# How the second product's columns are shared out over four column tiles of TensorE: 1, 2, 2, 1 matmuls in place of 1, 1, 1, 3

One core of one Trainium2 chip (trn2). The metric is the device time of the whole kernel in microseconds, from the first to the last instruction; lower is better. The run before takes 2520 us.

## The reference

A short causal convolution over time with one 7-tap filter for each of 8 heads, then a feed-forward block without bias, in fp32. The core of it:

```python
def reference(x, weight, w_in, w_out):        # x (8, 4096, 192), weight (8, 7)
    w = softmax(weight, axis=-1)
    out[b, s, h, g] = sum_k w[h, k] * x_pad[b, s + k, h, g]      # 6 zeros ahead of each sequence
    h = out.reshape(32768, 192) @ w_in                           # w_in (192, 2048)
    g = h * (1 / (1 + exp(-1.702 * h)))
    return g @ w_out                                             # w_out (2048, 192)
```

## The kernel before

It computes both matrix products by a Strassen-like scheme of sums and fewer block products. The work is cut in 64 stages of 512 tokens in two halves. Each stage has product 1 (with `w_in`), the activation on ScalarE, sums on VectorE, and then the second product: seven block products, each 96 output features (three chunks of 32) by 256 tokens, accumulated over 1024 rows of weights, 8 steps of 128.

TensorE is used as four column tiles of 128 x 32. A tile writes 32 partitions of PSUM, and one block product is 3 x 256 = 768 columns of 32 partitions, so 192 for each tile. The part that matters, cut and with comments added (`Q` = 32, `TA` = 192, `TB` = 64, `NK` = 8):

```python
def product2(slot, bank, a, b, first=True):
    dst = slot[:, bank, 0:TA]
    for j in range(NK):
        for c in range(3):                      # tiles 0, 1, 2: tokens 0 to 191 of chunk c
            nc.tensor.matmul(dst[c * Q : (c + 1) * Q, :],
                w_out_s[:, a, j, c * Q : (c + 1) * Q], g[:, b, j, 0:TA],
                start=(first and j == 0), stop=(j == NK - 1), skip_group_check=True)
        for c in range(3):                      # tile 3: tokens 192 to 255 of all three chunks
            nc.tensor.matmul(dst[3 * Q :, c * TB : (c + 1) * TB],
                w_out_s[:, a, j, c * Q : (c + 1) * Q], g[:, b, j, TA:T],
                start=(first and j == 0 and c == 0), stop=(j == NK - 1), skip_group_check=True)
    return dst

# ... in output(s, last, work): seven calls of product2, each followed by a copy on ScalarE
# or sums and 32 x 32 transposes on VectorE, then the transfers out:
for c in range(3):
    nc.sync.dma_start(out=rows[c, :, 0 : TA // Q, :], in_=osb[c * Q : (c + 1) * Q, n, :, :])
    nc.sync.dma_start(out=rows[c, :, TA // Q :, :],
                      in_=osb[3 * Q :, n, c * TB // Q : (c + 1) * TB // Q, :])
```

The call of `nc.tensor.matmul` loads its weights and multiplies. In fp32 each call shows up in the trace as two weight loads and two matmuls: 64 stages x 7 products x 8 steps x 6 calls are 21504 calls, and the trace has 43008 such matmuls. A "round" in all that follows is six matmuls of the trace, so there are 16 rounds in a block product and 112 in a stage.

## Time and profile before

| | before |
|---|---|
| median of 6 runs, us | 2520.47 (2517.91 to 2521.54) |
| span of the profiled run, us | 2520.6 |
| TensorE on the chain that ended last | 96% |
| second product on that chain | 47% |
| one stage of the second product, median | 18.90 us |

A stage of the second product is counted here from its first matmul to the first matmul of product 1 after it. The lines of the page and of the timeline are in the prediction. The end of the stage that the prediction reads, in the timeline of the kernel before (start in us, duration, engine, line):

```profile
1061.77 0.34 PE L445 MATMUL slot<-g,w_out_s 128*32 128x192 f32 x3
1061.80 0.50 PE L455 MATMUL slot<-g,w_out_s 128*32 128x64 f32 x6
1062.23 0.92 PE L350 MATMUL sums<-f,w_in_s 64*128 64x256 f32 x6
```

Tiles 0 to 2 are through with their last matmuls while tile 3 still has six of its own to go: three of the round before and three of the last. The stage ends with tile 3.

### The profile page before, as it was taken

To read this page: it belongs to the slowest core of one execution; us is meant where nothing else is said; L and a number is where in the kernel's file an instruction comes from. 1 tells how busy PE (TensorE), PEld (TensorE's weight loads), DVE (VectorE), ACT (ScalarE), POOL (GpSimd) and SP (SyncE) were. 2 spreads that over 40 slices of the span, in tenths; PEclk is the share of its full clock that TensorE was granted. 3 is DMA by queue.
4 is the path that set the end of the run, shared out by engine and by line. 5 is a ranking of instruction groups with operands and counts; after the bars stand their busy time and mean duration, and the time that the engine had idled before them with its cause. 6 is when DMAs were issued, how large, how long until landed. Compare 5 with 4: busy or idle time off the path is not lost.

```text
span 2520.6 us, 114341 instructions
## 1 busy us (share of the span) xinstructions
PE 2478.5 (98%) x54336; PEld 2303.3 (91%) x54336; DVE 1714.2 (68%) x2370; ACT 952.5 (38%) x1060; POOL 4.8 (0%) x20
## 2 busy tenths in 40 slices
PE   8889999999999999999999999999999999999998
PEld 5779999999999999999999999999999999999998
DVE  7856667666667666667666676666676666677654
ACT  6224334334334334334343343343343343343342
POOL 0000000000000000000000000000000000000000
PEclk9999999999999999999999999999999999999999
DMA  7122212212212222122122122122122222121110
GB/s 165 32 56 53 57 31 54 57 34 55 55 31 57 44 47 57 42 44 56 39 51 57 33 52 58 36 54 56 28 58 47 43 57 49 38 57 39 28 34 15
DMA packets 197603, 123.43 MB, mean 49 GB/s; under 512 B 115984, under 2 KB 191248, under 8 KB 193168
## 3 DMA queue, kind: packets, MB, share of 16 engines
q1 hardware_dynamic: 197120, 116.13, 21.9%
q8 instruction: 424, 6.95, 1.1%
q14 instruction: 43, 0.35, 0.0%
q10 hardware_dynamic: 16, 0.00, 0.0%
HBM read 53.15 MB, written 25.17 MB: 31 GB/s over the span
## 4 chain that ended last, share of the span: by engine, by line
PE 96%; DVE 1%; ACT 1%; DMA 1%; issue 0%; SPq 0%; DVEq 0%; ACTq 0%
PE slot L350 30%; PE slot L455 30%; PE sums L350 18%; PE slot L445 17%; PE slot L527 0%; DVE g L439 0%; ACT g L373 0%; DMA f<-f 0%; DMA xin<-in_x_dram 0%; ACT u L390 0%; DVE xt L296 0%; ACT f L198 0%; SPq L102 0%; ACT f L197 0%; ACT f L195 0%
## 5 line engine op out<-in xcount | busy, mean ns | idle before, releaser
L455 PE MATMUL slot<-g,w_out_s 128*32 128x64 f32 x21504 | 1219.6, 219 | 1.1 <-issue 0.8
L445 PE MATMUL slot<-g,w_out_s 128*32 128x192 f32 x21504 | 1209.6, 330 | 10.4 <-DVE w_out_s L257 9.9
L455 PEld LDWEIGHTS slot<-g,w_out_s 128*32 128x32 f32 x21504 | 1205.9, 110 | 2.7 <-issue 1.9
L350 PE MATMUL slot<-f,w_in_s 64*128 64x256 f32 x7168 | 843.9, 378 | 11.5 <-DMA f<-f 10.4
L350 PEld LDWEIGHTS slot<-f,w_in_s 64*128 64x128 f32 x7168 | 691.7, 188 | 100.5 <-DMA f<-f 11.2
L439 DVE TENSOR_TENSOR g<-g 128x1024 f32<-128x1024 f32 x512 | 609.5, 1222 | 191.9 <-ACT g L373 187.5
L445 PEld LDWEIGHTS slot<-g,w_out_s 128*32 128x32 f32 x21504 | 629.5, 108 | 34.2 <-issue 23.4
L350 PE MATMUL sums<-f,w_in_s 64*128 64x256 f32 x4096 | 515.1, 380 | 5.8 <-ACT sums L383 3.0
L390 ACT COPY u<-sums 128x1024 f32<-128x1024 f32 x128 | 129.5, 1012 | 1029.6 <-PE sums L350 1029.6
L350 PEld LDWEIGHTS sums<-f,w_in_s 64*128 64x128 f32 x4096 | 392.3, 187 | 56.7 <-ACT sums L383 3.7
L313 DVE SCALAR_TENSOR_TENSOR f<-xt,cw,f 128x512 f32<-128x512 f32 x558 | 417.5, 748 | 14.2
L373 ACT ACTIVATE g<-u 128x1024 f32<-128x1024 f32 x256 | 269.7, 1054 | 14.2 <-DVE u L430 14.1
L430 DVE TENSOR_TENSOR u<-u,slot 128x1024 f32<-128x1024 f32 x128 | 155.9, 1218 | 68.6 <-PE slot L350 68.6
L420 DVE TENSOR_TENSOR u<-u,slot 128x1024 f32<-128x1024 f32 x128 | 155.7, 1216 | 68.4 <-ACT u L403 65.5
L493 DVE TENSOR_TENSOR u<-u,slot 128x192 f32<-128x192 f32 x64 | 22.7, 355 | 247.7 <-PE slot L455 247.7
L403 ACT COPY u<-sums 128x1024 f32<-128x1024 f32 x128 | 129.6, 1012 | 133.7 <-PE sums L350 133.7
L373 ACT ACTIVATE g<-sums 128x1024 f32<-128x1024 f32 x128 | 130.6, 1020 | 94.7 <-PE sums L350 94.7
L373 ACT ACTIVATE g<-slot 128x1024 f32<-128x1024 f32 x128 | 131.5, 1027 | 45.0 <-PE slot L350 45.0
L383 ACT COPY sums<-slot 128x1024 f32<-128x1024 f32 x128 | 128.8, 1006 | 27.9 <-PE slot L350 25.8
L489 DVE TENSOR_TENSOR u<-u,slot 128x192 f32<-128x192 f32 x64 | 22.7, 354 | 99.6 <-PE slot L455 99.6
L483 ACT COPY u<-slot 128x192 f32<-128x192 f32 x64 | 20.4, 319 | 159.0 <-PE slot L455 159.0
L473 DVE STREAM_TRANSPOSE osb<-u 128x192 f32<-128x192 f32 x192 | 72.3, 376 | 4.4
(57 smaller groups left out, 417.5 us busy)
## 6 DMA issues: line engine op xcount, KB each, us to landing
xin<-in_x_dram SPq DMA_DIRECT2D x240, 180.0 KB, 4.5
f<-f SPq DMA_DIRECT2D x62, 576.0 KB, 4.8
out_dram<-osb SPq DMA_DIRECT2D x384, 48.0 KB, 1.7
out_dram<-osb SPq DMA_DIRECT2D x384, 16.0 KB, 1.5
g<-in_moe_w_in_dram SPq DMA_DIRECT2D x8, 384.0 KB, 9.4
g<-in_moe_w_out_dram SPq DMA_DIRECT2D x4, 768.0 KB, 5.1
xin<-in_x_dram SPq DMA_DIRECT2D x16, 160.0 KB, 3.2
f<-f SPq DMA_DIRECT2D x2, 256.0 KB, 3.4
```

Of the source, the lines that this page charges most:

```text
L313: vec.scalar_tensor_tensor(out=dst, in0=src, scalar=tap, in1=dst, op0=ALU.mult, op1=ALU.add)
L350: nc.tensor.matmul(slot[:, h, j * T : (j + 1) * T], w_in_s[halves[h], u, a, j * P : (j + 1) * P], f[halves[h], 0 if h == o else 1, b, :], ...
L373: act.activation(g[:, b, j : j + NK // NU, :].rearrange("p f t -> p (f t)"), src.rearrange("p h n -> p (h n)"), AF.Gelu_apprx_sigmoid,)
L383: act.copy(sums, self.x)
L390: act.copy(self.u2, sums)
L403: act.copy(self.u3, sums)
L420: vec.tensor_add(self.u3, self.u3, self.z)
L430: vec.tensor_add(self.u2, self.u2, self.z)
L439: vec.tensor_sub(v[dst], v[a], v[b])
L445: nc.tensor.matmul(dst[c * Q : (c + 1) * Q, :], w_out_s[:, a, j, c * Q : (c + 1) * Q], g[:, b, j, 0:TA], start=(first and j == 0), stop=(j ...
L455: nc.tensor.matmul(dst[3 * Q :, c * TB : (c + 1) * TB], w_out_s[:, a, j, c * Q : (c + 1) * Q], g[:, b, j, TA:T], start=(first and j == 0 a ...
L473: vec.transpose(osb[:, n, :, m * Q : (m + 1) * Q], src.rearrange("p (j t) -> p j t", t=Q),)
```

## The change

The 768 columns become one row, which is cut in four equal parts: a tile takes 192 consecutive columns. Two of the cuts fall inside a tile, so tiles 1 and 2 have two matmuls each, and no tile has three. The output transfers follow the new places.

```diff
-    TB = T - TA
+    # tile, chunk, first token, tokens, first column in the tile
+    LANES = [
+        (0, 0, 0, TA, 0),
+        (1, 0, TA, T - TA, 0),
+        (2, 1, T // 2, T // 2, 0),
+        (3, 2, T - TA, TA, 0),
+        (1, 1, 0, T // 2, T - TA),
+        (2, 2, 0, T - TA, T // 2),
+    ]
     for j in range(NK):
-        for c in range(3): ...  # 192 tokens of chunk c on tile c
-        for c in range(3): ...  # 64 tokens of chunk c on tile 3
+        for l, c, t, n, at in LANES:
+            nc.tensor.matmul(dst[l * Q : (l + 1) * Q, at : at + n],
+                w_out_s[:, a, j, c * Q : (c + 1) * Q], g[:, b, j, t : t + n],
+                start=(first and j == 0 and at == 0), stop=(j == NK - 1), skip_group_check=True)
```

(The diff is shortened: the removed calls are named by their comments, the comment on the fields is added here, and the transfers, cut away, loop over `LANES` in the same way.) The intent is that the slowest tile has less to do beside its columns.

More of the change, by code (lines that the diff above doesn't have):

```diff
@@ L443, in product2 @@
         for j in range(NK):
-            for c in range(3):
+            for l, c, t, n, at in LANES:
                 nc.tensor.matmul(
-                    dst[c * Q : (c + 1) * Q, :],
+                    dst[l * Q : (l + 1) * Q, at : at + n],
                     w_out_s[:, a, j, c * Q : (c + 1) * Q],
-                    g[:, b, j, 0:TA],
-                    start=(first and j == 0),
-                    stop=(j == NK - 1),
-                    skip_group_check=True,
-                )
-            for c in range(3):
-                nc.tensor.matmul(
-                    dst[3 * Q :, c * TB : (c + 1) * TB],
-                    w_out_s[:, a, j, c * Q : (c + 1) * Q],
-                    g[:, b, j, TA:T],
-                    start=(first and j == 0 and c == 0),
+                    g[:, b, j, t : t + n],
+                    start=(first and j == 0 and at == 0),
                     stop=(j == NK - 1),
@@ L507, in output @@
             rows = out_v[n, p, t : t + T, :].rearrange("(j i) (c e) -> c i j e", i=Q, e=2 * Q)
-            for c in range(3):
+            for l, c, t0, nt, at in LANES:
                 nc.sync.dma_start(
-                    out=rows[c, :, 0 : TA // Q, :], in_=osb[c * Q : (c + 1) * Q, n, :, :]
-                )
-                nc.sync.dma_start(
-                    out=rows[c, :, TA // Q :, :],
-                    in_=osb[3 * Q :, n, c * TB // Q : (c + 1) * TB // Q, :],
+                    out=rows[c, :, t0 // Q : (t0 + nt) // Q, :],
+                    in_=osb[l * Q : (l + 1) * Q, n, at // Q : (at + nt) // Q, :],
                 )
```

## The prediction

> **What bounds the kernel now.** I read the page's busy times first, then its chain of work, then the groups of the two lines that the change touches, and last the timeline of single stages.
>
> ```profile
> PE 2478.5 (98%) x54336; PEld 2303.3 (91%) x54336; DVE 1714.2 (68%) x2370; ACT 952.5 (38%) x1060; POOL 4.8 (0%) x20
> ...
> PE 96%; DVE 1%; ACT 1%; DMA 1%; issue 0%; SPq 0%; DVEq 0%; ACTq 0%
> PE slot L350 30%; PE slot L455 30%; PE sums L350 18%; PE slot L445 17%; PE slot L527 0%; DVE g L439 0%; ACT g L373 0%; DMA f<-f 0%; DMA xin<-in_x_dram 0%; ACT u L390 0%; DVE xt L296 0%; ACT f L198 0%; SPq L102 0%; ACT f L197 0%; ACT f L195 0%
> ...
> L455 PE MATMUL slot<-g,w_out_s 128*32 128x64 f32 x21504 | 1219.6, 219 | 1.1 <-issue 0.8
> L445 PE MATMUL slot<-g,w_out_s 128*32 128x192 f32 x21504 | 1209.6, 330 | 10.4 <-DVE w_out_s L257 9.9
> ```
>
> TensorE is on the chain for 96% of the span. Product 1 (L350) is 48% of it and the second product (L445 and L455) 47%, some 1185 us. The second product hardly waits for another engine: the one wait of size is 9.9 us at the start, for the rounded weights. So what the change is worth is the time in which TensorE streams one round of the second product, times the rounds: 43008 / 6 = 7168 rounds, 112 in each of 64 stages (7 products of 16). A round now is three matmuls of 192 columns, one each on column tiles 0 to 2 (L445), and three of 64 columns on tile 3 (L455).
>
> The mean duration of one matmul (330 and 219 ns) says nothing of the rate, since matmuls overlap. Starts do. The timeline at the start of the stage at 1043 us:
>
> ```profile
> 1043.33 0.36 PE L445 MATMUL slot<-g,w_out_s 128*32 128x192 f32 x3
> 1043.35 0.35 PE L455 MATMUL slot<-g,w_out_s 128*32 128x64 f32 x3
> 1043.52 0.34 PE L445 MATMUL slot<-g,w_out_s 128*32 128x192 f32 x3
> 1043.54 0.33 PE L455 MATMUL slot<-g,w_out_s 128*32 128x64 f32 x3
> 1043.68 0.34 PE L445 MATMUL slot<-g,w_out_s 128*32 128x192 f32 x3
> 1043.71 0.33 PE L455 MATMUL slot<-g,w_out_s 128*32 128x64 f32 x3
> 1043.84 0.34 PE L445 MATMUL slot<-g,w_out_s 128*32 128x192 f32 x3
> 1043.88 0.33 PE L455 MATMUL slot<-g,w_out_s 128*32 128x64 f32 x3
> 1044.01 0.34 PE L445 MATMUL slot<-g,w_out_s 128*32 128x192 f32 x3
> 1044.05 0.33 PE L455 MATMUL slot<-g,w_out_s 128*32 128x64 f32 x3
> 1044.17 0.34 PE L445 MATMUL slot<-g,w_out_s 128*32 128x192 f32 x3
> ```
>
> The first column is the start. L445 goes every 0.1625 us (1043.52 to 1044.17 in four rounds); L455 starts 0.02 us behind it in the second round and 0.04 in the fifth: tile 3 is slower and falls back. The same view late in the stage:
>
> ```profile
> 1056.08 0.34 PE L445 MATMUL slot<-g,w_out_s 128*32 128x192 f32 x3
> 1056.11 0.33 PE L455 MATMUL slot<-g,w_out_s 128*32 128x64 f32 x3
> 1056.24 0.35 PE L445 MATMUL slot<-g,w_out_s 128*32 128x192 f32 x3
> 1056.27 0.33 PE L455 MATMUL slot<-g,w_out_s 128*32 128x64 f32 x3
> 1056.41 0.34 PE L445 MATMUL slot<-g,w_out_s 128*32 128x192 f32 x3
> 1056.44 0.33 PE L455 MATMUL slot<-g,w_out_s 128*32 128x64 f32 x3
> ```
>
> Here L445 also goes every 0.165 to 0.17 us: it now [...] is held to tile 3's pace. From the single starts in the trace, L455 starts every 55.85 ns without a break from the second round to the last, so a round is 3 x 55.85 = 167.5 ns; L445, where nothing holds it, is at 162.5. From its first matmul to the first of the next product 1 (1062.23 in the timeline) the stage takes 18.90 us; 64 of them are 1210 us, in line with the chain's 47%.
>
> **What the Trainium skill says.** "TensorE: Matmul & The Clock Gate", section "Wait — 56ns, not 53.3ns?", has matmuls at N / 2.4 GHz plus about 2.5 ns each. The trace agrees if an fp32 column takes two clocks: 64 columns are 53.3 + 2.5 = 55.8 (55.85 seen), 192 are 160 + 2.5 = 162.5 (162.5 seen); the page's clock is granted too (0.994 over the run). So the three small matmuls on tile 3 pay the fixed cost three times. "TensorEngine Tiling (Array Packing)", section "Key Properties", says that different tiles load weights and multiply in parallel; the trace agrees, since 6 matmuls of 325 ns in all (2 x 162.5) would not fit in 167.5 otherwise. The first page's Part 3 ("The mechanism") says that matmuls keep program order in their starts. The trace differs: late in the stage L445 of a round starts some 36 ns before L455 of the round before. This is what lets the tiles drift apart.
>
> **The change, part by part.** Removed: nothing by count. Matmuls, weight loads (both 6 a round) and columns (768) stay; on VectorE, ScalarE and GpSimd the order of instructions is the same, and there are again 12 output transfers per stage with the same bytes, cut as 192, 64, 128, 192, 128, 64 columns. What moves is which tile takes which matmul. Per round:
>
> - tiles 0 and 3: one matmul of 192 columns, 162.5 ns.
> - tiles 1 and 2: one of 64 and one of 128. The latter is not in the trace; by the same rule it is 106.7 + 2.5 = 109.2 ns, an estimate from the two widths that are. Sum 55.85 + 109.2 = 165.05 ns.
>
> The longest tile sets the pace: 165.05 instead of 167.5, 2.45 ns a round. Times 112 it is 0.27 us a stage, times 64 it is 17.6 us. That lies wholly on the path, since TensorE sets the stage. The start of a stage gives little: today the second start on tile 3 comes 80 instead of 56 ns after the first, because its weight load is issued behind seven others; in the new order the second load on tile 1 is the fifth, some 7 ns each, so perhaps 7 ns a stage are saved, 0.4 us in all. The drain into product 1 (149 ns from the last start) stays. Sum: about -18 us, to 2500.4.
>
> Something is likely to be given back. Where L445 is held and then released, two rounds of its weight loads come together, the second 13 ns after the matmul that it should follow at 2 ns, and the next matmul then starts after 172.9 ns instead of 162.5: a late load delays the next matmul by as much. Today only tiles with slack pay this. In the new order two tiles are without slack, and the issue port serves one load about every 6.6 ns. I allow 0.2 to 0.3 ns a round on average, by judgement, some 2 us. Prediction: 2502.
>
> **The rivals.**
>
> 1. The sum of each tile's streaming times is all that counts (165.05, 2500). For it: tile 3 runs unbroken at 55.85 for a whole stage today, although 12 loads and matmuls of all tiles go out per round. Against it: only one tile was ever the slow one.
> 2. Late weight loads on tiles 1 and 2, which are now equally slow and alternate two widths. Were one such load (10.4 ns) lost every second round, a round would be 165.05 + 5.2 = 170.3, 2.8 more than today, and the time 2538; lost every round, 175.5 and 2576. For it: the case is seen in the trace, at L445. Against it: it is seen only there, where the tile ran ahead and was released late; tiles that lag have their loads queued in time, as tile 3's are (2 ns after each matmul). In the order 0, 1, 2, 3, 1, 2 the starts of tiles 1 and 2 come in program order by themselves.
> 3. A new bound elsewhere: VectorE or ScalarE no longer ready when TensorE comes 0.28 us earlier per stage, which would leave 2510 to 2518. Against it: VectorE is busy 9.0 of 18.75 us in this stage (stretch 1043.08 to 1061.83), ScalarE 3.2, and TensorE's waits for them are almost all in the first stages and the last.
> 4. The output's different cuts: at most the last transfers of the last stage are on the path, each 1.5 to 1.7 us to landing in both forms. Under 1 us.
>
> **Range and chances.** The first rival's 2500 is a floor but for the noise of the runs (2517.9 to 2521.0, 3 us), so 2498 below. Above, half of the gain lost is 2509, and a little more makes 2512. Over 2% faster would need 50 us, and the rule gives 18: 1%. Over 2% slower needs rival 2 in nearly every round: 4%. Within 2%: 95%.
>
> **What would show it.** In the changed profile: the one line of the second product in place of two, with 43008 matmuls, and 18.6 us from its first matmul to the first of product 1 in an undisturbed stage, not 18.90; by form 128 columns beside 64 and 192; starts of 64 and 128 on one tile 55.8 and 109.2 ns apart; rounds of 165.0 to 165.5 in steady state. Rounds at 170 with loads more than 2 ns behind their matmuls would show rival 2; new waits of TensorE for VectorE or ScalarE in every stage rival 3. The prediction is wrong if the 128-column matmul isn't on the rule, or if tiles 1 and 2 hold each other up in the queue.

## The result and the profile after

| | before | after |
|---|---|---|
| median, us (6 runs each) | 2520.47 | 2506.57 (2502.69 to 2508.86) |
| ratio | | 0.9944, 95% interval 0.9931 to 0.9957 |
| one stage of the second product, median | 18.898 us | 18.611 us |

A ratio here is the mean time of one kernel's fast runs over that of the other's of the same rounds, so not quite the ratio of the medians. All runs in this document were in the fast state but for the single run of one experiment, whose state is unknown; the granted clock was 0.993 to 0.995 in all profiles. The time fell by 13.9 us: within 2%, and within the range.

The changed page's chain by line, and the groups by form (count, then busy us and mean ns of one, then the idle time before them):

```profile
PE slot L456 47%; PE slot L360 30%; PE sums L360 18%; PE slot L525 0%; DVE g L449 0%; ACT g L383 0%; DMA f<-f 0%; SPq L510 0%; ACT u L400 0%; DVE diag L519 0%; ACT f L208 0%; ACT f L205 0%; ACT f L207 0%; ACT f L209 0%; DVE u L430 0%
```

```profile
L456 PE MATMUL slot<-g,w_out_s 128*32 128x128 f32 x14336 | 1201.8, 273 | 0.5 <-issue 0.5
L456 PE MATMUL slot<-g,w_out_s 128*32 128x192 f32 x14336 | 1199.8, 327 | 11.5 <-DVE w_out_s L267 9.9 <-DVE osb L474 1.1 <-issue 0.5
L456 PE MATMUL slot<-g,w_out_s 128*32 128x64 f32 x14336 | 1199.7, 220 | 1.1 <-issue 1.0
```

The second product is one line now, in three widths of equal count, and still 47% of the chain: nothing else has become the bound. The chain in order of time, in an undisturbed stage (start, us, what):

```profile
1115.28 18.61 PE slot L456 x339
1133.89 1.06 PE sums L360 x8
```

18.61 us, against 18.90 in the kernel before. In the single starts of the changed trace, matmuls on tile 1 follow 56, 109, 110 and 55 ns after each other (64, 128, 128 and 64 columns in turn): 330 ns for two rounds, so 165.0 a round. Taken over all stages the medians differ by 0.287 us, which in the 63 stages after the first is 18.1 us, the whole of the sum that the prediction worked out. Yet the spans differ by only 15.5 us (2520.6 and 2505.1). The rest shows where a stage is disturbed:

```profile
1040.96 12.10 PE slot L456 x220
1053.06 0.04 issue
1053.10 4.29 PE slot L456 x75
1057.39 1.11 PE sums L360 x8
```

In the middle of a block TensorE stops, and the weight loads show for how long and on what:

```profile
1052.57 0.27 PEld L456 LDWEIGHTS slot<-g,w_out_s 128*32 128x32 f32 x8
1053.10 0.50 PEld L456 LDWEIGHTS slot<-g,w_out_s 128*32 128x32 f32 x19 [0.26 <-issue]
```

0.26 us of idleness before the load at 1053.10, put down to "issue": it waited for nothing that the profile shows. I summed, over the stages after the first, how far each is over the median stage. That is 5.4 us before and 8.3 us after. With 18.1 us gained in the streaming, 2.9 lost here and 0.4 gained in the first stage, the difference of the second product is 15.6 us; this closes the account of the spans to 0.1 (what comes before the first second product is 1.1 us shorter, product 1 in all 1.1 us longer, and the two cancel).

What are these pauses? In both traces I numbered all of TensorE's instructions (loads, matmuls and the 47 semaphore waits and drains) in order of their starts. There are 21 gaps of over 140 ns inside the second product in each (from 150 us on), and all 42 come at the same place: after number 192 modulo 256. The instruction queue moves 424 packets of 16 KB in both:

```profile
q8 instruction: 424, 6.95, 1.1%
```

"Runtime: NRT & Kernel Launch", section "Instruction fetch mechanics", in the Trainium skill says that instructions are refilled in blocks of 16 KiB, 256 instructions, the next while the current one runs. The trace agrees in the size: 6.95 MB in 424 packets, one for every 256 of 108672 loads and matmuls. So a pause looks like a block of instructions that comes late. The packets bear this out: paired with the blocks in order of time, the packet of a late block has ended 1.2 to 1.6 us before the block begins, in both traces, and in no trace of this case does a block begin sooner than 1.18 us after its packet's end. How a block gets late can be followed too. While the second product runs, fetches start some 3.7 us apart (median 3.73 us before and 3.74 after, where both starts lie in one stage), but 256 instructions last less, 3.56 us before and 3.52 after. Counting the blocks that lie wholly in one stage, the fetch starts 0.32 us after the beginning of the block ahead of it in the first of the changed kernel's stage, then 0.48, 0.71, 0.92 and 1.02; 0, 1, 6, 14 and 3 of the blocks that were fetched so (of 63, 63, 63, 63 and 16) came late; three of these 24 lie before 150 us. Product 1 uses instructions slowly and gives the lead back. So the second product runs close to the rate at which its instructions come, and a gain in its pace should bring it closer.

That is two claims, one on the pace and one on the pauses, and both were put to the test.

### The profile page after: what moved, and what is told of

The parts are those of the page before. It is cut to its first block, busy times and chain, and to the rows that moved or that the text cites. A ratio compares the mean times of both kernels' runs of the same rounds, so it can differ in the third digit from the quotient of the medians.

```text
span 2505.1 us, 114341 instructions
## 1 busy us (share of the span) xinstructions
PE 2461.3 (98%) x54336; PEld 2285.7 (91%) x54336; DVE 1714.1 (68%) x2370; ACT 952.4 (38%) x1060; POOL 4.8 (0%) x20
## 3 DMA queue, kind: packets, MB, share of 16 engines
q8 instruction: 424, 6.95, 1.2%
## 4 chain that ended last, share of the span: by engine, by line
PE 96%; DVE 1%; ACT 1%; issue 0%; DMA 0%; SPq 0%; DVEq 0%; ACTq 0%
PE slot L456 47%; PE slot L360 30%; PE sums L360 18%; PE slot L525 0%; DVE g L449 0%; ACT g L383 0%; DMA f<-f 0%; SPq L510 0%; ACT u L400 0%; DVE diag L519 0%; ACT f L208 0%; ACT f L205 0%; ACT f L207 0%; ACT f L209 0%; DVE u L430 0%
## 5 line engine op out<-in xcount | busy, mean ns | idle before, releaser
L456 PEld LDWEIGHTS slot<-g,w_out_s 128*32 128x32 f32 x43008 | 1188.0, 110 | 39.8 <-issue 27.2
L456 PE MATMUL slot<-g,w_out_s 128*32 128x192 f32 (+2 forms) x43008 | 1204.7, 273 | 13.0 <-DVE w_out_s L267 9.9
L494 DVE TENSOR_TENSOR u<-u,slot 128x192 f32<-128x192 f32 x64 | 22.7, 355 | 245.3 <-PE slot L456 245.3
L490 DVE TENSOR_TENSOR u<-u,slot 128x192 f32<-128x192 f32 x64 | 22.6, 354 | 94.1 <-PE slot L456 94.1
L306 DVE STREAM_TRANSPOSE xt<-xin 128x576 f32<-128x576 f32 x96 | 67.2, 750 | 0.4 <-DMA out_dram<-osb 0.3
L501 DVE TENSOR_TENSOR u<-u,slot 128x192 f32<-128x192 f32 x64 | 22.7, 354 | 48.0 <-PE slot L456 48.0
```

The costliest lines, as they stand in the source:

```text
L306: vec.transpose(xts[big][:, c, :, :].rearrange("p n (j t) -> p (n j) t", t=Q), xins[big].rearrange("p n j d -> p (n j) d")[:, :, c * R : c ...
L456: nc.tensor.matmul(dst[l * Q : (l + 1) * Q, at : at + n], w_out_s[:, a, j, c * Q : (c + 1) * Q], g[:, b, j, t : t + n], start=(first and j ...
```

## The experiments

Theory A: a tile's time for a round is the sum over its matmuls of the streaming time (two clocks a column) and 2.5 ns each; the slowest tile sets the round. Theory B: instructions come at one block of 256 in some 3.7 us, and the pauses are late blocks. Rivals: the order of issue makes the difference, not the count on a tile; late weight loads eat part of the gain; all tiles move together; the pauses have another cause.

### The split of before in a mixed order

```diff
-        (0, 0, 0, TA, 0), (1, 0, TA, T - TA, 0), (2, 1, T // 2, T // 2, 0),
-        (3, 2, T - TA, TA, 0), (1, 1, 0, T // 2, T - TA), (2, 2, 0, T - TA, T // 2),
+        (3, 0, TA, T - TA, 0), (0, 0, 0, TA, 0), (3, 1, TA, T - TA, T - TA),
+        (1, 1, 0, TA, 0), (3, 2, TA, T - TA, T // 2), (2, 2, 0, TA, 0),
```

> The split of the kernel before (1, 1, 1 and 3 matmuls on the tiles), but issued in turn: tile 3, 0, 3, 1, 3, 2. Theory (a tile's pace is the sum of its streaming times, columns / 1.2 GHz + 2.5 ns each, and the slowest tile sets the round): 167.5 ns a round as before, 18.90 us a stage, time within 0.3% of before. Rival (the gain of the change comes from the issue order, in which no tile gets two matmuls in a row): 165 ns a round and some 14 us less than before. Supply of instructions: still 12 a round, so pauses like those of before.

2526.75 us, ratio 1.0029 (1.0014 to 1.0043), result correct. There is no gain, so the order is not what helps. In steady state tile 3 starts a matmul every 55.8 ns as before: its 48 starts in a block product span 2.624 us in both. But the stage is longer:

```profile
1505.99 19.01 PE slot L456 x337
1582.41 19.01 PE slot L456 x337
```

19.01 us against 18.90. The first to the last start takes 18.754 us (18.748 before); the rest of the difference is behind the last start, since the last call is now one of 192 columns and not of 64, and product 1 has to wait for it: 256 ns from the last start in place of 149, and 107 ns is also what 192 columns stream longer than 64 (162.5 and 55.8). 0.11 us in 64 stages is 7.2 us, about the 0.3% that the run is slower. That I had not expected. The pauses of this trace, at the pace of before, come to 2.5 us over the median stage, where the trace of before had 5.4: two traces at one pace can differ by 3 us.

### The changed split with each tile's matmuls together

```diff
-        (0, 0, 0, TA, 0), (1, 0, TA, T - TA, 0), (2, 1, T // 2, T // 2, 0),
-        (3, 2, T - TA, TA, 0), (1, 1, 0, T // 2, T - TA), (2, 2, 0, T - TA, T // 2),
+        (1, 0, TA, T - TA, 0), (1, 1, 0, T // 2, T - TA), (2, 1, T // 2, T // 2, 0),
+        (2, 2, 0, T - TA, T // 2), (0, 0, 0, TA, 0), (3, 2, T - TA, TA, 0),
```

> The changed split (1, 2, 2, 1), but with the two matmuls of a tile next to each other: tile 1, 1, 2, 2, 0, 3. Theory of the sums: 165.0 ns a round and 18.61 us a stage, as in the changed kernel, ratio to before about 0.9944. Rival (late weight loads: the second load of a tile without slack waits behind others of its own tile): 170 ns a round or more, 2538 us or more.

2508.23 us, ratio 0.9957 (0.9942 to 0.9972), correct: the gain is there within the noise. First to last start 18.480 us, against 18.462 in the changed kernel; the stage 18.66 against 18.61, again with a call of 192 columns at its end. 0.018 us in 112 rounds is 0.2 ns a round: late loads don't cost 5 even in this order, and that rival falls. (Pauses: 7.0 us over the median stage.)

### Fewer columns on the tiles with one matmul

```diff
+    MM = [(l, c, t, n - Q if n == TA else n, at) for l, c, t, n, at in LANES]
-            for l, c, t, n, at in LANES:
+            for l, c, t, n, at in MM:
```

> Wrong result on purpose: the changed kernel with the 192-column matmuls on tiles 0 and 3 cut to 160 columns (135.8 ns by the rule). Theory of the sums: these tiles have slack already, so the round stays at 165.0 ns, the median stage at 18.61 us and the time at that of the changed kernel within 0.2%. Rival (all four tiles move in step, or share something in proportion to the columns): the round falls by up to 64/768 of 165, 14 ns, and the time by tens of us.

2503.79 us, ratio 0.9937 (0.9922 to 0.9952), beside 0.9942 for the changed kernel in the same rounds. The chain of a stage:

```profile
1565.64 18.61 PE slot L457 x392
1603.44 18.61 PE slot L457 x392
```

A sixth of the columns of tiles 0 and 3 is gone and the stage doesn't move: these tiles have slack, and nothing is shared in proportion to columns. (Pauses: 5.3 us over the median stage.)

### Three columns fewer on the tiles with two

```diff
+    MM = [(l, c, t, n - 3 if n == T // 2 else n, at) for l, c, t, n, at in LANES]
-            for l, c, t, n, at in LANES:
+            for l, c, t, n, at in MM:
```

> Wrong result on purpose: the changed kernel with the 128-column matmuls on tiles 1 and 2 cut to 125 columns. Theory of the sums: tiles 1 and 2 then take 165.05 - 2.5 = 162.55 ns, level with tiles 0 and 3 (162.5), so a round is 162.5 and the median stage 0.28 us shorter than in the changed kernel, 18.33 us, 18 us in all. But 256 instructions then last 3.47 us, so the late ones grow: 2490 to 2495 us. Rival (tiles 0 and 3 also set the pace today, through the order of issue): under half of the shortening of the stage.

2492.72 us, ratio 0.9892 (0.9875 to 0.9908). Stages of one stretch:

```profile
1526.06 18.44 PE slot L457 x338
1563.69 18.33 PE slot L457 x336
1601.23 18.39 PE slot L457 x336
```

The shortest stages are at the 18.33 us expected, 0.28 under the changed kernel, from 3 columns in 192 on two of the four tiles. The others are longer by varying amounts, and the median is 18.40: 256 instructions last 3.47 us here, and late blocks are more frequent (28 gaps of over 140 ns). Counted over the shortest stage, since the median is itself disturbed, the stages lose 11.2 us, against 8.0 and 5.8 in the two traces of the changed kernel. The run agrees with both theories.

### One wide matmul on each tile with two

```diff
+    WIDE = TA + 3
+    MM = [(0, 0, 0, TA, 0), (1, 0, 0, WIDE, 0), (2, 1, 0, WIDE, 0), (3, 2, 0, TA, 0)]
-            for l, c, t, n, at in LANES:
+            for l, c, t, n, at in MM:
```

(The output is addressed as `slot[l * Q : (l + 1) * Q, bank, at : at + n]`, since 195 columns do not fit in `dst`.)

> Wrong result on purpose: the two matmuls on tile 1 become one of 195 columns with one set of weights, and so on tile 2; 4 matmuls and 4 loads a round. By the sums 195 / 1.2 + 2.5 = 165.0 ns a round, as in the changed kernel. If the pauses of TensorE in the middle of blocks (8.3 us over the median stage in the changed kernel's trace, about 5.4 in the trace before) are late instructions, they are gone, since 256 instructions last 5.3 us: 2497 to 2500 us, ratio to before about 0.991, and every stage at 18.6 us. If the pauses have another cause they stay and the time is that of the changed kernel, 0.9944.

2496.49 us, ratio 0.9910 (0.9893 to 0.9926), the four runs within 0.5 us of each other. Three stages in a row:

```profile
1523.57 18.61 PE slot L463 x442
1561.38 18.61 PE slot L463 x442
1599.18 18.61 PE slot L463 x442
```

The same pace as in the changed kernel, and no stage after the first is more than 50 ns over the median (20 were in the changed kernel). The instruction packets are 312:

```profile
q8 instruction: 312, 5.11, 0.9%
```

So the pauses go with the number of instructions at an equal pace of streaming, as theory B has it. (This run alone can't tell fewer instructions from fewer loads and matmuls; the place modulo 256 and the packets do. Here every block begins 3.7 us or more after its packet's end.) Against the changed kernel it is 8 us by the ratios, of the size of the pauses in its traces (8.3 us in the first, 5.7 in the second).

### One matmul of 192 columns on each tile

```diff
+    MM = [(0, 0, 0, TA, 0), (1, 0, 0, TA, 0), (2, 1, 0, TA, 0), (3, 2, 0, TA, 0)]
-            for l, c, t, n, at in LANES:
+            for l, c, t, n, at in MM:
```

> Wrong result on purpose: one matmul of 192 columns on each tile, 4 a round. By the sums 162.5 ns a round, 18.33 us a stage, and no late instructions: 18 us under the four-matmul form of 165 ns, so 2480 to 2482 us, ratio to before about 0.984. It is the floor for this split of the columns. If the pace does not follow the sum, it comes out at the time of the form with 195 columns.

2479.55 us, ratio 0.9846 (0.9832 to 0.9859), and 17 us less than with 195 columns.

```profile
1551.33 18.34 PE slot L457 x448
1588.86 18.34 PE slot L457 x448
```

This is the floor of 192 columns a tile. It isn't a version to use, for a matmul has one set of weights and two tiles need two.

### Two matmuls on every tile

```diff
+    MM = [
+        (0, 0, 0, T // 2, 0), (1, 0, TA, T - TA, 0),
+        (2, 1, T // 2, T // 2, 0), (3, 2, T - TA, T // 2, 0),
+        (0, 0, T // 2, T - TA, T // 2), (1, 1, 0, T // 2, T - TA),
+        (2, 2, 0, T - TA, T // 2), (3, 2, TA, T - TA, T // 2),
+    ]
-            for l, c, t, n, at in LANES:
+            for l, c, t, n, at in MM:
```

> The changed kernel with the matmuls of tiles 0 and 3 also cut in two (128 and 64 columns): 2, 2, 2, 2, right result, 8 matmuls and 8 loads a round. Theory of the sums alone: 165.05 ns a round on every tile, no change, about 2506 us. Rival (supply of instructions: 256 instructions come about every 3.74 us while the second product runs, as the pauses in the two traces suggest): 16 instructions a round make 234 ns a round once the lead gained in product 1 is used up, so a stage of 25 to 26 us in place of 18.6 and a time of 2900 to 2980 us.

2849.73 us (a single run, so its state is unknown; the result is correct). Who waited for whom, on TensorE's matmuls (total us, times, longest):

```profile
PE slot L466 <- issue: 264.1, 338, 1.4
PE slot L370 <- DMA f<-f: 10.9, 2, 10.6
```

By the sums of the tiles nothing should have changed. Instead TensorE waits 264 us for nothing that the profile shows. The chain of one stage, after a first stretch at full pace:

```profile
1136.07 2.84 PE slot L466 x96
1139.54 2.84 PE slot L466 x96
1143.02 2.84 PE slot L466 x96
1146.76 2.84 PE slot L466 x96
```

Work of 2.84 us, then a gap, every 3.47 to 3.75 us; from the second whole block of a stage on, the median of 256 instructions is 3.73 to 3.75 us. The 355 gaps of over 140 ns, 339 us in all, are again each behind number 192 modulo 256. The block begins 1.2 to 1.6 us after the end of its packet in these gaps too. Theory B is confirmed in its cause, but its time was 50 to 130 us too high: a stage took 24.2 us in place of the 25 to 26 estimated, because the first block of a stage (3.01 us) is largely at full pace and I seem to have taken the lead from product 1 too small.

### The changed kernel again

> The changed kernel again, beside the three kernels that are cut from it, to have its time in the same rounds and a second profile: ratio to before about 0.9944, median stage 18.61 us, round 165.0 ns. Its pauses fall at other places than in the first profile if they are late instructions that depend on the phase of the fetches, but again after every 256th instruction alone.

2504.79 us (2500.58 to 2507.17), ratio 0.9942 (0.9928 to 0.9955).

```profile
1983.21 18.61 PE slot L456 x337
2021.01 18.73 PE slot L456 x337
2058.94 18.61 PE slot L456 x337
```

The stage is the same to the nanosecond in the median (18.611 us), and the pauses are fewer and mostly elsewhere: 5.7 us over the median, 15 gaps, 3 of them where the first trace has one, and all behind the same number modulo 256. The runs spread over 6.6 us, those with four matmuls a round over 0.5 and 2.7.

## Why the prediction was right

- **The bound and the unit.** Right: TensorE's pace in the second product, times the rounds. One slip: the text has "7 products of 16", while the loop has 8 steps, each of which is two rounds in the trace. The count of rounds, 7168, was taken from the trace and is right. Another: six matmuls of a round one after the other would take 3 x 162.5 + 3 x 55.85 = 655 ns, not 325; that tiles work in parallel follows all the more.
- **The pace of a tile.** Right: 165.05 ns a round was an estimate with a width that no trace had shown, and the trace has 165.0. The median stage fell by 287 ns, 280 of it in the rounds, where 274 for the rounds and 7 for the start were worked out. The cuts confirm which tiles set the pace. The 7 ns at the start came, but not for the reason given: on tile 1 the second matmul still starts 80 ns after the first. What shortens the start is that the tile that ends the stage now has its first matmul at 13 ns and not at 20. That term was right by luck.
- **What is given back.** The sum had 2 us for late weight loads, "by judgement". The step that failed is that term: late loads cost nothing that can be seen in the undisturbed stages. By the ratios the gain is 14.1 and 14.6 us and not 18, so 3 to 4 us are missing, with an uncertainty of some 3 us; that 2 us were near is luck. What the runs show in the place of late loads is late blocks of instructions. But these cost 5.4 us in the trace of before as well, and only their growth counts: 2.9 us in the first pair of traces, 0.3 with the second trace of the changed kernel. The four traces at the new pace with six matmuls a round (5.3 to 8.3 us) lose more on average than the two at the old (2.5 and 5.4), but by no more than traces at one pace differ. So late blocks are shown as what stops TensorE; that they make up what is missing is not shown. In the trace of before they stood as "issue" in the waits, and I passed over them as noise.
- **The rivals.** Sums alone (2500): right for the median stage, but 4 to 7 us below the measured medians, and it has no supply of instructions in it. Late loads (2538 or more): didn't happen, and grouping the matmuls did not bring it on. Another engine as the bound: no, 47% of the chain is the second product as before. The output's cuts: no effect was looked for by itself; from the last matmul to the end the two traces take 7.20 and 7.24 us.

What stays open: what sets the 3.7 us between fetches, and so whether anything in a kernel could shorten it. With eight matmuls a round a packet takes some 1.1 us, and the block begins some 1.4 us after its end; the rest is not explained. No version was found that gives the right result and beats the changed kernel; with three chunks of 256 columns on four tiles, six matmuls are the fewest unless one tile takes a whole chunk. One was left untried: 193 columns on tiles 0 and 3 and 191 on tiles 1 and 2 would by the same sums take 164.2 ns a round (an estimate from 162.5 and 165.0), if the 32 x 32 transposes behind it allow such a cut.

## What to carry to other kernels

When matmuls run side by side on tiles of TensorE, add up each tile's streaming times with the fixed cost of every matmul, and level the slowest tile; equal columns are not equal time (three small ones cost 5 ns more a round than one large, 2.5 of which the change got back). Then ask how long 256 instructions of TensorE last: where it is under some 3.75 us for several blocks on end, a split into more matmuls can cost far more than it levels, and a faster pace may in part be given back. Idleness put down to "issue" deserves the same look as a wait with a name, and the last matmul before a switch to other work should be a short one (0.11 us a stage here).

## What the Trainium skill lacked or had wrong

- "Runtime: NRT & Kernel Launch", section "Instruction fetch mechanics", says that the crossing of a 16 KiB boundary is "mostly hidden". For TensorE that holds here with 12 loads and matmuls in 165 to 167.5 ns (2.5 to 8.3 us of pauses in the whole run), and no longer with 16 (339 us). It lacks a rate: fetches came 3.7 us apart under this load, so about 14.5 ns an instruction.
- "TensorE: Matmul & The Clock Gate", Part 3, has the starts of matmuls in program order. In the trace of before, matmuls of tile 0 started some 36 ns ahead of matmuls of tile 3 from earlier calls.
- The same page, section "Wait — 56ns, not 53.3ns?", has N / 2.4 GHz + 2.5 ns. The fixed cost holds for each matmul of a column tile (55.85 ns for 64 columns, 162.5 for 192), but the section does not say how fp32 enters this rule: each fp32 call was two matmuls of two clocks a column.
- No page has a time for the change from column tiles to row tiles: 149 ns from the start of the last matmul, with 64 columns, to the first of product 1, and up to 0.11 us more with 192 columns in that place.
